# A fused attention and Fourier-mixing kernel: first-norm arithmetic moved to GpSimd, score products and loads of the first batch reordered, five filler matmuls added

## The chip, the cores and the metric

The kernel runs on one core of one Trainium2 chip. The metric is device time in microseconds (us) of one launch. Ten runs of the kernel before lie between 835.83 and 841.03 us, with a median of 837.63 us. One execution, of 836.47 us, was also profiled; the instructions in its trace span 834.7 us, and all the positions named below ("at 52.67 us") count from the start of that span.

## The reference

Four batches of 768 tokens, eight heads of 64. Each token attends to its neighbours closer than 16 tokens and to 24 block summaries (the maximum of 32 keys, the mean of 32 values). The heads side by side are a row of 512 numbers, x. Then a Fourier mix, a norm, and a two-layer network with hidden width 2048. Cut to what matters:

```python
k_sum = k.reshape(B, H, nb, 32, D).max(axis=3)
v_sum = v.reshape(B, H, nb, 32, D).mean(axis=3)
scores = concat([where(|i - j| < 16, q @ k.T / 8, -1e9), q @ k_sum.T / 8 + log(32)])
x = softmax(scores) @ concat([v, v_sum])          # to (B, S, H*D)
u = x + real(fft(fft(x, axis=1), axis=2))
un = (u - mean(u)) / sqrt(var(u) + 1e-6)          # over the 512 numbers of a row
out = u + relu(un @ w_ch1) @ w_ch2                # w_ch1, w_ch2 come as float64
```

## The kernel before

All matmuls are 32-bit, and each stands in the trace as two records, except transposes, which stand as one. The work goes batch by batch, and the tensor engine (PE) is the engine that is nearly always busy.

**First attention.** Batch 0 has nothing to overlap with, so its attention is written out by hand: inside `first_attention` the order of PE and VectorE (DVE) is the order of the code. Its eight heads are four pairs g = 0..3. For a pair, `prepare` transposes keys and queries (tiles `kn`, `qn`) into `kt`, `qt`, and DVE reduces the keys to block maxima `km` (L698). `wide_scores` multiplies twelve windows of 96 keys by 64 queries, in two halves of six windows; in each half the six windows of both heads come first, then the block maxima (L718), then the exponentials on ScalarE (ACT, L720) and a mask product on DVE. `wide_values` multiplies by the values `vw` (L741); DVE divides, and the halves of the sequence are folded (`fold_sequence`, `fold_halves`, `fold_ends`), which is the input of the Fourier stage. The PSUM banks are in two pools of four, `abank` and `bank`. Scores, sums of values and `av` use `abank`; transposes of batch 0 use `bank`.

**Loads.** Nearly every load goes through `fetch`, that is through SyncE's one queue (SP), in program order; a load that waits holds back all behind it. In `first_attention`, after pair 0, the queue gets the values of pair 2, the Fourier tables `fs` (two parts) and `fd` (L1016), then the values of pair 3 (`vw`, six loads of small pieces), then at g = 1 a first piece of the float64 weights (`words`), the keys and queries of batch 1, and another piece of weights.

**First Fourier stage.** `gen_fourier(0)` does the sequence transform (tiles `y`, L1072 and L1076; tables `fs`) and the channel transform (`mx`, L1100 and L1102; table `fd`), six row tiles. For each half of the rows (three tiles) DVE takes mean and variance (L1107, L1108) and then the inverse square root by a bit trick and three Newton steps, on tiles of 128x3: L1120 to L1132, fourteen DVE instructions for each half, all dependent. Then each row tile is scaled (`un`, L1144 on ACT or L1147 on DVE), transposed by PE (`unt`, L1151) and copied to `u` (L1152), and `_right_sums` makes four more operands from it. From these `gen_hidden` (tiles `hx`, `hy`, `hz`, L1173) makes the hidden layer by a seven-product scheme, and `gen_out` the output.

**Beside it.** A scheduler orders the instructions of all that runs together: `drive` mixes the Fourier stage with the conversion of the weights (`convert`, L929 to L939: DVE and ACT turn float64 words into float32, four raw pieces in flight, each freed by L936) and with the attention of batch 1 (`scores`, L757; `values`, L780 to L795). Block sums of values for batch 1 are loaded and added in `block_sums(1, 0)` (L1330; eight partial sums by additions and a DVE reduction, L623). The Fourier stage has priority 600 over the rest. For later batches the norm uses the same Newton lines, on DVE.

Of the kernel before, what the change touches and what calls it, by code (L numbers as in the profile page):

```python
# [10 lines left out]
I32 = mybir.dt.int32  # L11
# [5 lines left out]
P = 128  # L17
# [401 lines left out]
QB = 64  # L419
# [68 lines left out]
def _main_program(ctx, tc, q, k, v, moe_w_ch1, moe_w_ch2, out):  # L488
# [64 lines left out]
    def abank(shape, name):  # L553
        return psum.tile(shape, FP, tag="attn", bufs=4, name=name)
# [6 lines left out]
    def tt(out, in0, in1, op):  # L561
        nc.vector.tensor_tensor(out=out, in0=in0, in1=in1, op=op)  # L562

    def gtt(out, in0, in1, op):
        nc.gpsimd.tensor_tensor(out=out, in0=in0, in1=in1, op=op)
# [18 lines left out]

    def add_blocks(gg):
        raw, vb = to_add[gg]
        n = BLOCK * D // 2
        while n > D:
            tt(raw[:, 0:n], raw[:, 0:n], raw[:, n:2 * n], ADD)
            n //= 2  # L590
        tt(vb, raw[:, 0:D], raw[:, D:2 * D], ADD)

    def block_sums(b, gg):

        heads, rows = slice(4 * gg, 4 * gg + 4), 4 * nb
        f = BLOCK // 4
        n = f * D
        vb = spool.tile([rows, D], FP, tag="vbs", bufs=2, name=f"vbs_{b}_{gg}")
        for g in (2 * gg, 2 * gg + 1):
            sums[b, g] = vb, sel[:, g % 2]  # L600
        src = v[b, heads].rearrange("h (n f) d -> (h n) (f d)", f=BLOCK)
        if b == 0:

            raw = words[0:rows, 4 * n * gg:4 * n * (gg + 1)]
            fetch(out=raw, in_=src)
            to_add[gg] = raw, vb
            return
        if done_weights:
            raw = room(f"vb_{b}_{gg}")
            raw = [raw[0:rows, n * i:n * (i + 1)] for i in range(4)]  # L610
        else:

            raw = [bpool.tile([P, NC, P], FP, tag="s", bufs=5, name=f"vb_{b}_{gg}_{i}").rearrange("p n t -> p (n t)")
                   [0:rows] for i in range(4)]
        for i in range(4):
            fetch(out=raw[i], in_=src[:, n * i:n * (i + 1)])

        add = gtt if done_weights else tt
        add(raw[0], raw[0], raw[1], ADD)
        add(raw[2], raw[2], raw[3], ADD)  # L620
        add(raw[0], raw[0], raw[2], ADD)
        if not done_weights:
            nc.vector.tensor_reduce(out=vb, in_=raw[0].rearrange("p (f d) -> p d f", d=D), op=ADD, axis=AX.X)  # L623
        else:
            while f > 2:
                f //= 2
                gtt(raw[0][:, 0:f * D], raw[0][:, 0:f * D], raw[0][:, f * D:2 * f * D], ADD)
            gtt(vb, raw[0][:, 0:D], raw[0][:, D:2 * D], ADD)

# [72 lines left out]
    def wide_scores(b, g, between=None):  # L704

        kt, km, qt = kt_bufs[g % 2], km_bufs[g % 2], nat[b, g]
        p = apool.tile([P, 2, NQ, QB], FP, tag="p", name=f"p_{b}_{g}")
        for half in range(2):
            n0, n1 = NQ // 2 * half, NQ // 2 * (half + 1)
            ps = [abank([P, NQ // 2, QB], f"sc_{b}_{g}_{half}_{e}") for e in range(2)]  # L710
            for n in range(n0, n1):
                for e in range(2):
                    rows = slice(D * e, D * (e + 1))
                    nc.tensor.matmul(ps[e][0:WK, n - n0, :], kt[rows, QB * n:QB * n + WK],
                                     qt[rows, QB * n:QB * (n + 1)], start=True, stop=True)
            for e in range(2):
                rows = slice(D * e, D * (e + 1))
                nc.tensor.matmul(ps[e][WK:P], km[rows, :], qt[rows, QB * n0:QB * n1], start=True, stop=True)  # L718
            for e in range(2):
                nc.scalar.activation(out=p[:, e, n0:n1], in_=ps[e], func=AF.Exp, scale=SC)  # L720
                tt(p[:, e, n0:n1], p[:, e, n0:n1], wide[:, None, :].to_broadcast([P, NQ // 2, QB]), ALU.mult)
            if half == 0 and between:
                between()
        return p

    def sum_values(b, g):

        ps = abank([P, 2, D], f"vs_{b}_{g}")
        for e in range(2):
            vb, pick = sums[b, g]  # L730
            nc.tensor.matmul(ps[WK:P, e], pick[:, D * e:D * e + 32], vb, start=True, stop=True)

        (nc.vector.tensor_copy if g in (0, NP - 1) else nc.scalar.copy)(
            out=wide_vw(g)[WK:P, :, :, 0:D], in_=ps[WK:P, :, None, :].to_broadcast([P - WK, 2, NQ, D]))

    def wide_values(b, g, p, x):
        vw = wide_vw(g)
        av = [abank([P, NST, D1], f"av_{b}_{g}_{e}") for e in range(2)]
        for n in range(NQ):
            for e in range(2):  # L740
                nc.tensor.matmul(av[e][QB * (n % 2):QB * (n % 2 + 1), n // 2, :], p[:, e, n, :], vw[:, e, n, :],  # L741
                                       start=True, stop=True)
        for e in range(2):
            rc = rec[:, b * NP + g, e]
            nc.vector.reciprocal(out=rc, in_=av[e][:, :, D])
            tt(x[:, :, P * g + D * e:P * g + D * (e + 1)], av[e][:, :, 0:D],
               rc[:, :, None].to_broadcast([P, NST, D]), ALU.mult)
# [63 lines left out]
    def first_attention():  # L811
# [8 lines left out]
        for g in range(NP - 1):  # L820
            p[g + 1] = wide_scores(0, g + 1, (lambda: add_blocks(1)) if g == 1 else None)
            wide_values(0, g, p[g], x)
            load_values(*following(0, g, 2))
            for par in range(2):
                fold_sequence(par, g)
            if g == 0:
                get_tables(0)
            if g < NP - 2:
                prepare(0, g + 2)
                sum_values(0, g + 1)  # L830
            if g == NP - 3:
                load_raw(1)
                load(1, 0)
                load_raw(2)
                sum_values(0, g + 2)
        fold_halves(0, 0)
        wide_values(0, NP - 1, p[NP - 1], x)
# [166 lines left out]
    def get_tables(b):  # L1004
        tag, bufs = ("w1", 3) if b else ("w2", NC)
        fs = []
        for par in range(2):
            t = bpool.tile([P, 2, HT, F2 + 1], FP, tag=tag, bufs=bufs, name=f"fs_{b}_{par}")
            fetch(out=t, in_=dr["fs"].ap()[par])
            fs.append(t)  # L1010
        if b:
            fd = bpool.tile([P, C["fm"].shape[1]], FP, tag=tag, bufs=bufs, name=f"fm_{b}")
            fetch(out=fd, in_=dr["fm"].ap())
        else:
            fd = bpool.tile([P, 6, HD], FP, tag=tag, bufs=bufs, name=f"fd_{b}")
            fetch(out=fd, in_=dr["fd"].ap())  # L1016
        tables[b] = fs, fd
        return fs, fd

    def mix_halves(ps, y, fm, xt, half):  # L1020

# [16 lines left out]
    def gen_fourier(b):  # L1038
        x = x_of[b]
        Q = DM // 4  # L1040
        fs, fd = tables[b] if b in tables else get_tables(b)


        bank = abank if b else dense_bank
# [40 lines left out]
        for half in range(2):  # L1085
# [5 lines left out]
            for i in range(HT):  # L1091
# [23 lines left out]
                                     accum_out=var[:, i:i + 1])  # L1115
                yield

            y, z = norm[:, 0], norm[:, 1]
            if b == 0:
                nc.vector.tensor_scalar(out=minus, in0=both[:, :, 0], scalar1=-1.0, scalar2=None, op0=ALU.mult)  # L1120
                nc.vector.tensor_scalar(out=var, in0=both[:, :, 1], scalar1=1e-6, scalar2=None, op0=ADD)
            else:
                nc.vector.tensor_scalar(out=var, in0=var, scalar1=1.0 / DM, scalar2=1e-6, op0=ALU.mult, op1=ADD)
            nc.vector.tensor_scalar(out=y.bitcast(I32), in0=var.bitcast(I32), scalar1=1, scalar2=None,
                                    op0=ALU.arith_shift_right)
            nc.vector.tensor_scalar(out=y.bitcast(I32), in0=y.bitcast(I32), scalar1=-1.0, scalar2=float(0x5F3759DF),
                                    op0=ALU.mult, op1=ADD)
            for _ in range(3):
                nc.vector.scalar_tensor_tensor(out=z, in0=y, scalar=-0.5, in1=y, op0=ALU.mult, op1=ALU.mult)
                tt(z, z, var, ALU.mult)  # L1130
                nc.vector.scalar_tensor_tensor(out=y, in0=z, scalar=1.5, in1=y, op0=ADD, op1=ALU.mult)
            ins = nc.vector.tensor_tensor(out=z, in0=minus, in1=y, op=ALU.mult)  # L1132
            if b == 0:
                marks["mx", 0] = ins.ins
            norms.append((y, z))
        issued.add(("mx", b))
        for j in range(3):
            get_w1(b, j)

        for t in range(NST):  # L1140
# [9 lines left out]
            for d in range(NDT):  # L1150
                nc.tensor.transpose(ps[:, d // 2, d % 2, :], un[:, t, P * d:P * (d + 1)], ident)  # L1151
            (nc.vector.tensor_copy if t % 2 else nc.scalar.copy)(  # L1152
                out=u[:, half:half + 3:2, :, P * i:P * (i + 1)], in_=ps)
            yield
        _right_sums(tt, lambda i: u[:, i])
        wt["u", b] = u
# [170 lines left out]
    nc.vector.memset(vs, 0.0)  # L1327
    nc.vector.tensor_scalar(out=vs[:, :, D], in0=half_of, scalar1=float(BLOCK), scalar2=None, op0=ALU.mult)

    block_sums(1, 0)  # L1330

    def second_attention():
        prepare(1, 0)
# [76 lines left out]
```

## Time and profile before

| what | value |
|---|---|
| median of ten runs | 837.63 us (835.83 to 841.03) |
| profiled execution | 836.47 us, trace span 834.7 us |
| PE busy in the span | 803.9 us (96%) |
| DVE / ACT / POOL (GpSimd) busy | 487.8 us / 254.9 us / 16.1 us |
| mean granted PE clock | 0.992 |
| PE busy from 200 us to 700 us | 493.7 of 500 us |
| PE busy from 40 us to 50 us | 3.95 of 10 us |
| DVE busy from 90 us to 130 us | 39.8 of 40 us |

How to read it: PE is the engine that bounds the kernel, so time is lost where PE waits or where its granted clock is below full. From 200 us on there is little of either. The lower rows are stages of the first 200 us, in which batch 0 has its attention, its Fourier stage and its norm, and the weights are converted.

### The profile page before, as it was taken

To read this page: it belongs to the slowest core of one execution; us is meant where nothing else is said; L and a number is where in the kernel's file an instruction comes from. 1 tells how busy PE (TensorE), PEld (TensorE's weight loads), DVE (VectorE), ACT (ScalarE), POOL (GpSimd) and SP (SyncE) were. 2 spreads that over 40 slices of the span, in tenths; PEclk is the share of its full clock that TensorE was granted. 3 is DMA by queue.
4 is the path that set the end of the run, shared out by engine and by line. 5 is a ranking of instruction groups with operands and counts; after the bars stand their busy time and mean duration, and the time that the engine had idled before them with its cause. 6 is when DMAs were issued, how large, how long until landed. Compare 5 with 4: busy or idle time off the path is not lost.

```text
span 834.7 us, 14698 instructions
## 1 busy us (share of the span) xinstructions
PE 803.9 (96%) x6074; PEld 577.2 (69%) x6074; DVE 487.8 (58%) x1117; ACT 254.9 (31%) x561; POOL 16.1 (2%) x27
## 2 busy tenths in 40 slices
PE   8968998999999999999999999999999999999997
PEld 5757655445578856886568875787667875786586
DVE  5778998977978553533376823542347833532352
ACT  3533756444635023203234313121323502101200
POOL 0010000000000200020000000000000000000000
PEclk9989999999999999999999999999999999999999
DMA  9997697978733277247542253523312135205001
GB/s 207 228 246 153 194 248 252 313 217 262 241 109 108 79 269 202 83 77 248 106 92 97 85 202 129 128 38 122 129 46 88 72 101 214 89 1 220 1 26 54
DMA packets 101612, 120.55 MB, mean 144 GB/s; under 512 B 50560, under 2 KB 83552, under 8 KB 101344
## 3 DMA queue, kind: packets, MB, share of 16 engines
q1 hardware_dynamic: 100848, 119.31, 48.7%
q8 instruction: 50, 0.82, 0.4%
q10 hardware_dynamic: 688, 0.20, 0.1%
q14 instruction: 26, 0.21, 0.1%
HBM read 96.96 MB, written 22.54 MB: 143 GB/s over the span
## 4 chain that ended last, share of the span: by engine, by line
PE 83%; DVE 9%; ACT 3%; DMA 3%; issue 1%; ACTq 0%; SPq 0%; DVEq 0%
PE hx L1173 18%; PE ox L1237 17%; PE hz L1173 9%; PE oz L1237 8%; PE y L1072 4%; PE o L1214 4%; PE hy L1173 4%; PE oy L1237 4%; PE mx L1029 2%; PE sc L757 2%; PE unt L1151 1%; DVE w L562 1%; PE y L1076 1%; PE av L790 1%; DMA vw<-in_v_dram 1%
## 5 line engine op out<-in xcount | busy, mean ns | idle before, releaser
L1173 PE MATMUL hx<-u,w 128*128 128x384 f32 x512 | 186.2, 491 | 7.8 <-DVE h L562 3.9
L1173 PEld LDWEIGHTS hx<-u,w 128*128 128x128 f32 x512 | 94.5, 190 | 72.7 <-DVE h L562 7.6
L1173 PE MATMUL hz<-u,w 128*128 128x384 f32 x256 | 93.3, 487 | 0.0
L1237 PE MATMUL ox<-w,s 128*128 128x256 f32 x336 | 81.5, 381 | 0.3
L1237 PE MATMUL oz<-w,s 128*128 128x256 f32 x336 | 80.7, 379 | 0.0
L1237 PE MATMUL ox<-w,h 128*128 128x256 f32 x336 | 78.4, 381 | 0.4 <-DVE x L562 0.4
L1173 PEld LDWEIGHTS hz<-u,w 128*128 128x128 f32 x256 | 48.4, 190 | 34.3 <-ACT h L1190 1.1
L562 DVE TENSOR_TENSOR x<-ox,x 128x256 f32<-128x256 f32 x84 | 35.4, 423 | 62.0 <-PE ox L1237 61.9
L1237 PEld LDWEIGHTS ox<-w,h 128*128 128x128 f32 x336 | 63.2, 190 | 11.1 <-DVE x L562 1.5
L1237 PEld LDWEIGHTS oz<-w,s 128*128 128x128 f32 x336 | 63.5, 190 | 8.4
L1237 PEld LDWEIGHTS ox<-w,s 128*128 128x128 f32 x336 | 62.5, 190 | 9.2 <-DVE x L562 1.1
L562 DVE TENSOR_TENSOR h<-hx,h 128x384 f32<-128x384 f32 x32 | 17.8, 557 | 67.4 <-PE hx L1173 67.4
L1183 ACT COPY h<-hx 128x384 f32<-128x384 f32 x32 | 15.3, 477 | 127.3 <-PE hx L1173 115.6
L562 DVE TENSOR_TENSOR h<-hy,h 128x384 f32<-128x384 f32 x32 | 17.8, 557 | 60.6 <-PE hy L1173 57.4
L1173 PE MATMUL hy<-u,w 128*128 128x384 f32 x128 | 46.6, 487 | 0.0
L1214 PE MATMUL o<-w,h 128*128 128x512 f32 x96 | 42.6, 596 | 1.2 <-DVE w L562 1.2
L1237 PE MATMUL oy<-w,h 128*128 128x256 f32 x168 | 39.8, 379 | 0.0
L1199 ACT ACTIVATE h<-hx 128x384 f32<-128x384 f32 x32 | 15.7, 489 | 79.2 <-PE hx L1173 79.2
L1072 PE MATMUL y<-fs,fold 128*128 128x193 f32 x192 | 37.9, 344 | 0.1
L1072 PEld LDWEIGHTS y<-fs,fold 128*128 128x128 f32 x192 | 32.0, 195 | 6.3 <-issue 4.9
L1173 PEld LDWEIGHTS hy<-u,w 128*128 128x128 f32 x128 | 24.2, 190 | 17.1 <-DVE w L562 0.6
L1237 PEld LDWEIGHTS oy<-w,h 128*128 128x128 f32 x168 | 31.9, 190 | 4.3
(141 smaller groups left out, 1075.0 us busy)
## 6 DMA issues: line engine op xcount, KB each, us to landing
w<-dw SPq DMA_DIRECT2D x44, 896.0 KB, 5.8
words<-in_moe_w_ch_dram SPq DMA_DIRECT2D x32, 512.0 KB, 6.1
dw<-w SPq DMA_DIRECT2D x12, 896.0 KB, 7.3
vw<-in_v_dram SPq DMA_DIRECT2D x47, 192.0 KB, 5.4
kn<-in_k_dram SPq DMA_DIRECT2D x16, 384.0 KB, 4.8
qn<-in_q_dram SPq DMA_DIRECT2D x16, 384.0 KB, 5.6
out_dram<-x SPq DMA_DIRECT2D x24, 256.0 KB, 2.2
fs<-c_fs SPq DMA_DIRECT2D x8, 579.0 KB, 3.6
```

The lines of the kernel that those rows point to most:

```text
L562: nc.vector.tensor_tensor(out=out, in0=in0, in1=in1, op=op)
L757: nc.tensor.matmul(ps[h][r:r + 64, i, :], kt[rows, o:o + 64], qt[rows, o:o + BLOCK], start=True, stop=True)
L790: nc.tensor.matmul(av[r][32 * j:32 * (j + 1), t, :], p[rows, h, i - NB2 * h, :], vw[rows, i, :], start=(t == 0), stop=False, skip_group_ch ...
L1029: nc.tensor.matmul(out, y[:, g], table, start=True, stop=last, skip_group_check=True)
L1072: nc.tensor.matmul(y, fgs[par][:, st, P * g:P * (g + 1)], fs[par][:, g % 2, st, :], start=(st == 0), stop=(st == HT - 1))
L1076: nc.tensor.matmul(ps[0:1, par:par + F2 + 1], zq[:, par, s2:s2 + 1], fs[par][:, 0, s2, :], start=False, stop=False, skip_group_check=True)
L1151: nc.tensor.transpose(ps[:, d // 2, d % 2, :], un[:, t, P * d:P * (d + 1)], ident)
L1173: nc.tensor.matmul(ps, w[:, a, kk, :], u[:, r, kk, :], start=start and kk == 0, stop=stop and kk == 1, skip_group_check=True)
L1183: nc.scalar.copy(out=c11, in_=X)
L1199: nc.scalar.activation(out=c21, in_=X, func=AF.Relu)
L1214: nc.tensor.matmul(ps, h[:, n, hf, P * t:P * (t + 1)], wt[2, b, j][:, 2 * hf:2 * hf + 2, :], start=(n, hf) == (0, 0), stop=(n, hf) == (NC ...
L1237: nc.tensor.matmul(ps, left[a][:, n, :], wt[2, b, j][:, r, :], start=start and n == 0, stop=stop and n == NC - 1, skip_group_check=True)
```

## The change

Six things change; the arithmetic of the result is the same.

1. In `wide_scores` the window products of both halves come first, then the block maxima of both halves. All four `abank` banks are taken at once; so `sum_values` and `wide_values` take theirs from `bank`.
2. At g = 1 of `first_attention` the order of the loads is new: keys and queries of batch 1, two pieces of weights, the four raw block-sum tiles of batch 1, and then the table `fd`, which was ahead of the values of pair 3. These loads now stand in the code ahead of the preparation of pair 3. The additions of those block sums stay where they were in the code, in `add_blocks(2)`.
3. Block sums on DVE are a tree of additions to the end; the reduction L623 is gone.
4. In the Newton lines of batch 0 all but the integer shift goes to GpSimd. A step is now four instructions rather than three, for later batches too, where it stays on DVE.
5. Two matmuls of the identity by a 128x512 tile stand behind the norms, and three more behind the transposes of the third row tile; nothing reads their result.
6. In the order that the scheduler makes of it, nine more score products of batch 1 go ahead of `y`; the rest of the first pair's attention of batch 1, which lay between the norms and the transposes of `un`, comes after the last of these transposes.

```diff
@@ add_blocks, block_sums
+        add = gtt if done_weights else tt
+        if isinstance(raw, list):
+            add(raw[0], raw[0], raw[1], ADD)
+            add(raw[2], raw[2], raw[3], ADD)
+            add(raw[0], raw[0], raw[2], ADD)
+            raw, n = raw[0], n // 4
+        while n > 2 * D:
             n //= 2
-        tt(vb, raw[:, 0:D], raw[:, D:2 * D], ADD)
+            add(raw[:, 0:n], raw[:, 0:n], raw[:, n:2 * n], ADD)
+        add(vb, raw[:, 0:D], raw[:, D:2 * D], ADD)
...
-            nc.vector.tensor_reduce(out=vb, in_=raw[0].rearrange("p (f d) -> p d f", d=D), op=ADD, axis=AX.X)
...
+        to_add[2] = raw, vb
+        if now:
+            add_blocks(2)
@@ wide_scores
+        ps = [[abank([P, NQ // 2, QB], f"sc_{b}_{g}_{half}_{e}") for e in range(2)] for half in range(2)]
+        for n in range(NQ):
+            half, i = divmod(n, NQ // 2)
+            for e in range(2):
+                rows = slice(D * e, D * (e + 1))
+                nc.tensor.matmul(ps[half][e][0:WK, i, :], kt[rows, QB * n:QB * n + WK],
+                                 qt[rows, QB * n:QB * (n + 1)], start=True, stop=True)
         for half in range(2):
...
-                nc.tensor.matmul(ps[e][WK:P], km[rows, :], qt[rows, QB * n0:QB * n1], start=True, stop=True)
+                nc.tensor.matmul(ps[half][e][WK:P], km[rows, :], qt[rows, QB * n0:QB * n1], start=True, stop=True)
@@ sum_values, wide_values
-        ps = abank([P, 2, D], f"vs_{b}_{g}")
+        ps = bank([P, 2, D], f"vs_{b}_{g}")
...
-        av = [abank([P, NST, D1], f"av_{b}_{g}_{e}") for e in range(2)]
+        av = [bank([P, NST, D1], f"av_{b}_{g}_{e}") for e in range(2)]
@@ first_attention
             if g == 0:
                 get_tables(0)
+            elif g == 1:
+                load(1, 0)
+                load_raw(2)
+                block_sums(1, 0, False)
+                get_channel_table(0)
             if g < NP - 2:
                 prepare(0, g + 2)
                 sum_values(0, g + 1)
             if g == NP - 3:
-                load_raw(1)
-                load(1, 0)
-                load_raw(2)
                 sum_values(0, g + 2)
@@ gen_fourier
+    def keep_busy(name, t, n):
+        ps = dense_bank([P, DM], name)
+        for _ in range(n):
+            nc.tensor.matmul(ps, ident, t, start=True, stop=True)
...
+            eng = nc.vector if b else nc.gpsimd
...
-                nc.vector.tensor_scalar(out=minus, in0=both[:, :, 0], scalar1=-1.0, scalar2=None, op0=ALU.mult)
-                nc.vector.tensor_scalar(out=var, in0=both[:, :, 1], scalar1=1e-6, scalar2=None, op0=ADD)
+                eng.tensor_scalar(out=minus, in0=both[:, :, 0], scalar1=-1.0, scalar2=None, op0=ALU.mult)
+                eng.tensor_scalar(out=var, in0=both[:, :, 1], scalar1=1e-6, scalar2=None, op0=ADD)
...
             for _ in range(3):
-                nc.vector.scalar_tensor_tensor(out=z, in0=y, scalar=-0.5, in1=y, op0=ALU.mult, op1=ALU.mult)
-                tt(z, z, var, ALU.mult)
-                nc.vector.scalar_tensor_tensor(out=y, in0=z, scalar=1.5, in1=y, op0=ADD, op1=ALU.mult)
-            ins = nc.vector.tensor_tensor(out=z, in0=minus, in1=y, op=ALU.mult)
+                eng.tensor_tensor(out=z, in0=y, in1=y, op=ALU.mult)
+                eng.tensor_tensor(out=z, in0=z, in1=var, op=ALU.mult)
+                eng.tensor_scalar(out=z, in0=z, scalar1=-0.5, scalar2=1.5, op0=ALU.mult, op1=ADD)
+                eng.tensor_tensor(out=y, in0=y, in1=z, op=ALU.mult)
+            ins = eng.tensor_tensor(out=z, in0=minus, in1=y, op=ALU.mult)
...
+        if b == 0:
+            keep_busy("busy_0", x[:, NST - 1, :], 2)
...
+            if (b, t) == (0, HT - 1):
+                keep_busy("busy_1", un[:, t, :], 3)
@@ after first_attention
-    block_sums(1, 0)
+    add_blocks(2)
```

## The prediction

> **What bounds the kernel now.** I read the windows of busy time first. PE is busy 493.7 of 500 us from 200 to 700 us, so a gain has to come from the first 200 us. Columns: stretch, length, busy PE, PEld, DVE, ACT, POOL, granted clock, DMA share, GB/s.
>
> ```profile
> 40.00:50.00 10.00, 3.95 (x95) 3.50 (x91) 8.00 (x20) 1.29 (x4) 1.37 (x5) 0.98 0.99 226
> 50.00:60.00 10.00, 9.08 (x40) 7.19 (x41) 6.83 (x17) 4.88 (x13) 2.26 (x3) 0.67 1.17 241
> 80.00:90.00 10.00, 7.62 (x154) 6.46 (x156) 9.19 (x31) 7.65 (x15) 0.00 (x0) 0.83 0.87 224
> 120.00:130.00 10.00, 7.67 (x34) 4.95 (x33) 10.00 (x21) 7.73 (x16) 0.00 (x0) 1.00 1.08 214
> ```
>
> There are three losses: PE waits from 40 to 50, and then runs at a low clock; it waits and runs slowly from 80 to 90, at the norms; from 120 to 130 it waits with DVE full. PE's timeline, read next, names the waits (start, length, what, and in brackets the idle time before it and what ended it):
>
> ```profile
> 44.51 1.82 PE L741 MATMUL av<-vw,p 128*64 128x65 f32 x48 [3.35 <-DMA vw<-in_v_dram]
> 48.60 0.85 PE L694 MATMUL qk<-ident,kn 128*128 128x128 f32 x6 [2.27 <-DMA kn<-in_k_dram]
> 52.32 0.42 PE L757 MATMUL sc<-qt,kt 64*64 64x32 f32 x2 [0.92 <-ACT qt L696]
> ...
> 81.68 0.41 PE L780 MATMUL vs<-vbs,sel 96*128 96x64 f32 x2 [1.82 <-DVE norm L1126]
> ...
> 129.15 1.56 PE L1173 MATMUL hx<-u,w 128*128 128x384 f32 x4 [2.33 <-DVE h L562]
> ```
>
> The first two are late loads. SP's timeline says why:
>
> ```profile
> 34.00 0.43 SPq L549 DMA_DIRECT2D fd<-c_fd  x1
> ...
> 36.02 5.35 SPq L549 DMA_DIRECT2D vw<-in_v_dram  x1
> ...
> 43.30 0.50 SPq L549 DMA_DIRECT2D kn<-in_k_dram  x1
> ```
>
> `fd` stands ahead; the issue of a part of `vw` is then held 5.35 us, and `kn` is issued at 43.30 only. In the chain of waits from 32 to 60 us, that transfer (36.02, 8.36 us) is followed by `av`, by the folds on DVE from 48.37, and by `y` at 52.74.
>
> **The change, part by part.**
>
> *Loads and score order (+4.0 us).* Between the end of the third pair's `av` (41.17) and the first `y` (52.67) lie 11.5 us, in which PE does 3.6 us of work: `av` 1.7, transposes 1.5, scores 0.4. So 7.9 us are waits. After the change `fd` is behind `vw`, so I expect `vw` at 40 to 41 rather than 44.4. Keys and queries of batch 1 are issued near 40; loads of this stretch land 3.8 to 4.9 us after their issue, so near 44 to 45. The limit is then DVE's order: exponentials of the first halves start about 1.2 us later, as the second windows go ahead of them, but PE's waits for block maxima (0.58 us is one) go. The divisions of the last pair, which start at 46.27 now, I place at 44.8. The last fold ended at 49.85 and so ends at 48.4, and `qt` on ACT (eight copies of 0.52 us from about 43.5) is done by 48. `y` starts near 48.6: 52.67 − 48.6 ≈ 4.0. Bounds: 2 if the small pieces of `vw` and not `fd` hold the queue, 5 if DVE's order gives more. That `av` and block-sum products now share `bank` with transposes costs short waits for ACT's copies, taken in. `fd` itself, 8.3 us in flight in the trace, would land near 55 and is needed near 62; with that cover gone each us late is a us of wait.
>
> *Clock in `y` (0).* PE's clock is granted at half from 49.84 to 56.75 and costs about 1.9 us of `y`. PE would still be idle for much of 42.5 to 48.6, so I leave this loss: 0, bounds 0 and +1.9.
>
> *Newton steps on GpSimd.* The trace has no such chain there. For each half DVE does 14 dependent instructions of 0.13 to 0.17 us (0.07 of DVE's pace each), among large ones in order; from the last aggregate to the end it takes 8.2 us for the first half (73.98 to 82.2) and 7.9 for the second (78.9 to 86.86). POOL gets 16 for each half, 128x3, and the shift stays on DVE in its order. POOL's rows:
>
> ```profile
> L565 POOL TENSOR_TENSOR vb<-vb 96x512 f32<-96x512 f32 x6 | 8.3, 1394 | 232.1 <-DMA vb<-in_v_dram 231.9
> L565 POOL TENSOR_TENSOR vbs<-vb 96x64 f32<-96x64 f32 x2 | 0.6, 316 | 129.0 <-PE vs L780 129.0
> L868 POOL COPY zq<-fold 128x3 f32<-128x3 f32 x2 | 1.0, 490 | 2.4 <-DVE fold L562 2.4
> L866 POOL COPY fold<-fold 128x6 f32<-128x6 f32 x2 | 1.5, 761 | 6.2 <-DVE fold L562 6.2
> ```
>
> A line through 316 ns at 64 columns and 1394 at 512 gives 0.17 at 3 columns; 0.19 with a margin is the low bound. A dependent chain of additions of later block sums shows 0.08 more for each link. The copies of 3 columns, at the same width but beside a busy DVE, give 0.49, and the dearest copy of 6 columns 1.33: high bounds. The operation is nearest to the additions, the neighbourhood to the copies; I take 0.33, the low one with its link (0.27) and a little contention. Then, with T the end of `mx` (76.1 now, near 72 then): the last aggregate at T+3.3, two operations and the shift to T+4.3, 14 × 0.33 = 4.6 to T+9. The last transposes of `un` end T+10.2 to T+11.2. Queued behind: on POOL nothing that PE needs soon; on DVE the scaling of the first half's rows stands ahead of the last aggregate, so a late first norm delays the second.
>
> The Trainium skill ("GPSIMD Engine Reference", § 4.1 Engine selection) speaks against this part: elementwise work belongs on VectorE, and with two inputs it is about twice as slow on GpSimd. The trace agrees at 512 columns: 1.394 us there, 0.68 on DVE. By twice 0.16 us a step would be 0.32, and 14 of them 4.5 us, which is no other sum than mine.
>
> *Busy matmuls and the order at the norms (−3.3 us).* The same product as `o` of 128x512, 14 records in 6.25 us, is 0.446 a record; five matmuls are ten records, 4.46 us of PE. From T to the end of the transposes PE now has: the scores of one pair, 70 records at 0.017 (1.59 us for 94) = 1.2; busy 4.46; transposes, 24 at 0.13 = 3.1; together 8.7 of some 10.7 us, so 2.0 idle. After that the chain of exponentials and copies on ACT, moved here from under the norms, costs about 0.9. Lost: 4.46 + 2.0 + 0.9 = 7.4. Before, idle 2.5 (79.86 to 84.0) and half clock from 83.9 to 87.1, 1.6: 4.1. So −3.3, bounds −2 (POOL at 0.19) and −7 (0.53, with the clock falling too). What the fillers buy is the clock: without them 1.6 would stay lost and 4.46 be waits in part, so they are nearly free where POOL is slow.
>
> The Trainium skill ("TensorE: Matmul & The Clock Gate", Part 4) says that transposes don't count as busy for the clock. The trace has the clock at half during transposes at 84 to 87, but after a wait of 1.8 us, so it doesn't separate them. By that rule the three fillers among the transposes are needed, and without them the sum would be 1.6 lower.
>
> *DVE relieved (+3.5 us).* The block-sum work of batch 1 (three additions of 0.68 and the 1.02 reduction, 3.0 us) leaves the norm stage for DVE's gap from 50 to 60, where it is 6.83 busy. The tree costs 0.95 in place of 1.02: nothing. 26 Newton instructions off DVE at 0.07 are 1.8, plus the order's 0.7 or so: 5.5 us less on an engine that is 9.2 to 10 busy from 80 to 130. PE's waits for DVE and ACT between 94 and 153 are 0.21, 0.31, 1.17, 2.33 and 1.22, together 5.2. I take two thirds back; bounds +1 and +5. What comes late next is weights: pieces on SP's queue wait behind loads that PE frees, whose users now come after the transposes. The sixth and later pieces would be issued near 97.7, not 91.45, and land about when `hx` needs them (104); that is why not all returns.
>
> *Later batches (−0.6).* A step is four DVE instructions, not three: 3 more for each half, 18 in all, at 0.13 to 0.17 us in a chain that PE's other work covers mostly: bounds 0 and −1.5; about 0.03 each.
>
> Sum: 4.0 + 0 − 3.3 + 3.5 − 0.6 = +3.6. The profiled execution takes 836.47 (span 834.7 and 1.77 around it), so 832.9; the median is 1.16 above it: 834.0 us.
>
> **The rivals.**
>
> *Larger gain.* POOL at 0.19 (norm ready at T+7) and no low clock in `y`: 1.3 + 1.9 more than the forecast, and all 5.2 of the waits back, 1.5: 829.3. For it: DVE's own row for 128x3 is only 0.15, and the earlier `vw` shortens PE's gap. Against: POOL's small copies.
>
> *The loads don't do what they say.* The 5.35 us hold falls on the third part of `vw`, not the first: many small packets may hold the queue by themselves. Then the first term is 1 to 2, and the relief, which partly comes from the earlier end of `mx`, 2.5: 3.6 − 2.5 − 1 = +0.1, so 837.5, no change. For it: the stretch moves 226 GB/s, with DMA share 0.99, so what goes ahead of `vw` merely exchanges places with what goes behind.
>
> *Slower: the Newton chain on POOL becomes the wait.* Its place is between the last aggregate and the scaling of the second half. Each 0.1 us an operation moves it by 1.4 us. The gain of 3.6 is used up at 0.33 + 3.6/14 = 0.59; with the clock falling again (1.6) at 0.47. At 0.53 it is 2.8 + 1.6 = 4.4 against 3.6: 838.4; if DVE's relief is then useless too, 841.9; at 1.33, 14 × 1.0 = 14 and the clock: near 850. For it: the 0.49 copies. Against: they ran while DVE folded with strided tiles, and the other 6-column copy took 0.20.
>
> **How the numbers follow.** About 0.3%, 2.5 us, is what a measurement of this kernel can tell from no change: 835.1 to 840.1 counts as same. Forecast 0.45 (own range 831 to 837), larger gain 0.17, loads without effect 0.18, slower chain 0.20. Faster: most of the first (0.35) and all of the second, 0.52. Same: 0.10 of the first, 0.13 of the third and 0.04 of the fourth, 0.27. Slower: 0.16 of the fourth and 0.05 of the third, 0.21. The range reaches from the larger gain to the mild end of the chain: 828.5 to 840.5.
>
> **What would show it.** In the changed kernel's profile: `vw` landing near 41 and `y` starting near 48.6 (still at 51 or later: the loads failed); clock 0.5 for some 6 us in `y`; Newton rows on POOL of about 0.25 to 0.35 each, the second norm near T+9, the last transposes by T+11; ten records of 0.45 us ahead of them, with the clock full there; the 2.33 us wait near 129 gone; PE as busy as before from 200 us on. POOL rows of 0.5 or more, PE waiting for `words` or `w` at 95 to 110, or PE waiting for `fd` at `mx`, would make the prediction wrong.

## The result, and the profile after

The changed kernel takes 842.78 us (median of 15 runs, 839.66 to 847.18); the kernel before, run beside it, 836.72 us (52 runs). The ratio is 1.0073, 95% interval 1.0055 to 1.009: slower by some 6 us, where the prediction said 3.6 us faster (834.0 us, range 828.5 to 840.5). The profiled execution took 840.97 us, with a span of 839.1 us (before: 834.7).

The windows of the changed kernel first (stretch, length, then busy PE, PEld, DVE, ACT, POOL, granted clock, DMA share, GB/s):

```profile
40.00:50.00 10.00, 6.34 (x131) 5.08 (x128) 9.26 (x24) 5.63 (x12) 1.31 (x5) 0.95 1.00 281
50.00:60.00 10.00, 10.00 (x43) 7.91 (x43) 8.69 (x21) 3.36 (x10) 2.26 (x3) 0.71 1.03 187
80.00:90.00 10.00, 7.74 (x59) 4.33 (x58) 6.58 (x12) 7.52 (x16) 2.26 (x10) 1.00 0.10 29
90.00:100.00 10.00, 8.95 (x216) 6.41 (x216) 8.01 (x18) 3.46 (x8) 0.00 (x0) 0.83 0.95 223
120.00:130.00 10.00, 9.81 (x121) 6.00 (x121) 10.00 (x24) 5.26 (x12) 0.00 (x0) 1.00 0.33 90
```

The first stretch is better, as foretold: 6.34 us of PE in place of 3.95. So is the last: 9.81 in place of 7.67. What is new lies between. From 80 to 90, VectorE has fallen from 9.19 to 6.58 us and the loads from 224 to 29 GB/s; from 90 to 100 the clock is at half for a time, where it was full before.

PE's timeline of the changed kernel, at the places that the prediction named:

```profile
40.56 3.07 PE L740 MATMUL av<-vw,p 128*64 128x65 f32 x96
...
49.67 2.91 PE L1087 MATMUL y<-fs,fold 128*128 128x193 f32 x8 [0.96 <-POOL fold L872]
...
75.45 1.98 PE L1031 MATMUL busy<-x,ident 128*128 128x512 f32 x4
77.68 1.59 PE L1171 MATMUL unt<-ident,big 128*128 128x128 f32 x12 [0.24 <-DVE both L1123]
79.11 2.74 PE L1031 MATMUL busy<-big,ident 128*128 128x512 f32 x6
83.93 1.53 PE L1171 MATMUL unt<-ident,big 128*128 128x128 f32 x12 [2.08 <-ACT big L1164]
...
85.64 0.85 PE L772 MATMUL ss<-qt,km 64*32 64x384 f32 x8
```

The two last `av` run as one block with no wait for `vw`; `y` starts at 49.67, not 52.67, with nine score products of batch 1 ahead of it (18 records; before it was one, so eight more and not nine). Behind `mx` come the fillers, a wait of 2.08 us for the second norm, and only after the transposes the block scores `ss` of the first pair of batch 1, which stood at 77.56 before.

The second norm itself is not late. Its chain on POOL, first and last lines of the timeline:

```profile
77.71 0.43 POOL L1137 TENSOR_SCALAR stat<-both 128x3 f32<-128x3 f32 x1 [0.76 <-DVE both L1123]
...
81.73 0.19 POOL L1146 TENSOR_TENSOR norm<-norm 128x3 f32<-128x3 f32 x1
82.00 0.19 POOL L1147 TENSOR_TENSOR norm<-norm,stat 128x3 f32<-128x3 f32 x1
...
82.83 0.20 POOL L1150 TENSOR_TENSOR norm<-stat,norm 128x3 f32<-128x3 f32 x1
```

Most operations are 0.19 to 0.20 us, and the next one starts 0.27 to 0.28 us after the start of such a one; a few take 0.3 to 0.5. From 78.72 (L1143) to 83.03 the 14 of the second half take 4.31 us, 0.31 a link. `mx` ends at 74.1 and the norm is ready at 83.0, 8.9 us later; the prediction had said 9.

A ledger over the span (PE's idle time; what half clock cost, as one less the granted clock, times busy time, summed over windows of 1 us; and the fillers) accounts for 3.9 of the 4.4 us between the two spans:

| profiled execution | span | PE idle | half clock | fillers | sum of the last three |
|---|---|---|---|---|---|
| before | 834.7 | 30.8 | 4.5 | 0 | 35.3 |
| changed | 839.1 | 28.2 | 6.5 | 4.5 | 39.2 |

PE waits 2.6 us less, but the fillers' 4.5 us came on top instead of lying in the waits, and half clock costs 2.0 us more.

### The profile page after: what moved, and what is told of

It reads as the page before. It is cut to its first block, busy times and chain, and to the rows that moved or that the text cites. A ratio compares the mean times of both kernels' runs of the same rounds, so it can differ in the third digit from the quotient of the medians.

```text
span 839.1 us, 14755 instructions
## 1 busy us (share of the span) xinstructions
PE 810.9 (97%) x6084; PEld 578.0 (69%) x6084; DVE 485.4 (58%) x1117; ACT 254.1 (30%) x561; POOL 24.5 (3%) x59
## 4 chain that ended last, share of the span: by engine, by line
PE 83%; DVE 7%; ACT 6%; issue 1%; POOL 1%; DMA 1%; DVEq 0%; ACTq 0%; POOLq 0%
PE hx L1195 18%; PE ox L1259 17%; PE hz L1195 9%; PE oz L1259 8%; PE y L1087 4%; PE hy L1195 4%; PE oy L1259 4%; PE o L1236 3%; PE mx L1042 2%; PE sc L756 2%; ACT kt L694 2%; ACT qt L694 2%; DVE x L562 1%; PE y L1091 1%; PE qk L684 1%
## 5 line engine op out<-in xcount | busy, mean ns | idle before, releaser
L1195 PEld LDWEIGHTS hz<-u,w 128*128 128x128 f32 x256 | 48.5, 190 | 34.6 <-ACT h L1212 1.4
```

The lines of the kernel that those rows point to most:

```text
L1195: nc.tensor.matmul(ps, w[:, a, kk, :], u[:, r, kk, :], start=start and kk == 0, stop=stop and kk == 1, skip_group_check=True)
```

## The experiments

All times are medians beside runs of the kernel before on the same chip; the ratios carry 95% intervals. A hundredth of a per cent is 0.08 us.

| kernel | median us | ratio to before |
|---|---|---|
| changed | 842.78 | 1.0073 (1.0055 to 1.009) |
| e1 no fillers | 841.18 | 1.0068 (1.0042 to 1.0095) |
| e2 Newton on VectorE | 833.50 | 0.9961 (0.9938 to 0.9984) |
| e3 neither fillers nor GpSimd | 837.16 | 1.0001 (0.9976 to 1.0026) |
| e4 old score halves | 844.59 | 1.0107 (1.007 to 1.0143) |
| e5 conversion behind the shift | 840.56 | 1.005 (1.0027 to 1.0073) |
| e6 order on PE | 841.13 | 1.0063 (1.0043 to 1.0083) |
| e7 before, with fillers | 836.27 | 0.9994 (0.9974 to 1.0013) |
| e8 Newton on VectorE, three instructions | 840.24 | 1.0046 (1.0025 to 1.0066) |
| e9 order on PE, ScalarE, VectorE | 832.98 | 0.9966 (0.9948 to 0.9985) |
| e10 Newton on VectorE, no fillers | 834.87 | 0.9982 (0.9967 to 0.9998) |
| e11 e2 again | 832.49 | 0.9954 (0.9939 to 0.9969) |
| e12 edges on ScalarE alone | 835.45 | 0.9987 (0.9966 to 1.0009) |
| e13 e9 with old loads | 839.24 | 1.0035 (1.001 to 1.006) |
| e14 e9 with old score halves | 833.88 | 0.9991 (0.9969 to 1.0014) |
| e15 e9, three instructions later | 834.88 | 0.9977 (0.9954 to 1.0001) |

### First: which part costs the time (e1 to e4)

e1 takes the five fillers out:

```diff
-        if b == 0:
-            keep_busy("busy_0", x[:, NST - 1, :], 2)
...
-            if (b, t) == (0, HT - 1):
-                keep_busy("busy_1", un[:, t, :], 3)
```

> The changed kernel without the five dense matmuls; all else kept. Three theories for the 6.1 us (836.7 to 842.8). F (fillers): their 4.46 us of PE are paid whole, and they push the first pair's attention of batch 1 out of the wait for the norms; without them that attention stands in the wait again: 837 to 838.5, and the time from the end of mx to the first hx shrinks though the clock may fall to half there. N (Newton steps on GpSimd are the loss): 842 to 844, as the wait for the second norm stays and the clock falls. A (first attention: a 1.4 us wait on issue at 26 and the half clock behind it, 28 to 31): 842 or more.

e2 puts the Newton steps back on VectorE:

```diff
-            eng = nc.vector if b else nc.gpsimd
+            eng = nc.vector
```

> The changed kernel with the Newton steps of batch 0 back on VectorE (still four instructions a step), fillers kept. F: the fillers still cost, but now stand in a longer wait with part of the first pair's attention: 841 to 843.5. N: 837 to 839. A: 842 to 843.5.

e3 does both, with the three-instruction step of before:

```diff
-                eng.tensor_tensor(out=z, in0=y, in1=y, op=ALU.mult)
-                eng.tensor_tensor(out=z, in0=z, in1=var, op=ALU.mult)
-                eng.tensor_scalar(out=z, in0=z, scalar1=-0.5, scalar2=1.5, op0=ALU.mult, op1=ADD)
-                eng.tensor_tensor(out=y, in0=y, in1=z, op=ALU.mult)
+                nc.vector.scalar_tensor_tensor(out=z, in0=y, scalar=-0.5, in1=y, op0=ALU.mult, op1=ALU.mult)
+                tt(z, z, var, ALU.mult)
+                nc.vector.scalar_tensor_tensor(out=y, in0=z, scalar=1.5, in1=y, op0=ADD, op1=ALU.mult)
```

> The changed kernel with neither fillers nor Newton steps on GpSimd (three instructions a step on VectorE, as before): what is left is the order of loads and scores and the tree. F: the 3.0 us by which y starts earlier remain, part of it lost again at the VectorE waits: 833.5 to 836. N: the same, 833.5 to 836. A: 838 or more, as the wait at 26 and the half clock at 28 to 31 remain.

e4 undoes the order of the score halves and the PSUM pools that go with it:

```diff
-        ps = [[abank([P, NQ // 2, QB], f"sc_{b}_{g}_{half}_{e}") for e in range(2)] for half in range(2)]
...
         for half in range(2):
+            ps = [abank([P, NQ // 2, QB], f"sc_{b}_{g}_{half}_{e}") for e in range(2)]
...
-        av = [bank([P, NST, D1], f"av_{b}_{g}_{e}") for e in range(2)]
+        av = [abank([P, NST, D1], f"av_{b}_{g}_{e}") for e in range(2)]
```

> The changed kernel with the score halves in the old order (block maxima and exponentials of the first half ahead of the windows of the second, PSUM pools as before); loads, Newton steps and fillers kept. F and N: 841.5 to 844, y starting within 1 us of the changed kernel's. A: 838.5 to 840, with no wait on issue near 26 and the clock full at 28 to 31.

My first theory was the fillers. It fell: without them 841.18 us. The first attention fell too (e4 is no faster). Newton on VectorE, one line, gave 833.5 us, which is faster than the kernel before; e11, the same program again, confirmed it (832.49). So the loss goes with the place of the Newton steps. But how? Their operations had taken 0.31 us a link, and the norm had been ready when foretold.

Two of these runs say something of the loads too. e3 is in substance the kernel before with the new loads, the new order of scores and the tree. Its `y` starts at 50.37, 2.3 us earlier than before, and its time is the same as before (1.0001), where 833.5 to 836 was expected, or 838 and more by the third theory: an earlier `y` alone gave nothing that shows at the end. And in e4 the wait for `vw` is back, with `fd` behind `vw`, and `y` starts at 52.14, against the expectation for it:

```profile
44.03 3.07 PE L739 MATMUL av<-vw,p 128*64 128x65 f32 x48 [2.99 <-DMA vw<-in_v_dram]
```

The six loads of `vw` hold the queue for 7.43 us there, from 34.91; in the changed kernel it is 5.93 us, from 33.54. Why they took longer in e4 is open; e14 below has the same loads and score halves and waits 0.18 us.

### Second: by what means (e5 to e8)

The program's order of instructions is made by a scheduler from the durations that it assumes, and with Newton on GpSimd it set the transposes of `un`, and what feeds them, ahead of the rest of the first pair's attention. Three causes were to be told apart: the weight conversion, which was queued on VectorE behind the last Newton step and was free once that step had left VectorE (M); the order on PE (O); GpSimd itself (P).

e5 queues the conversion behind the shift, which stayed on VectorE:

```diff
-            nc.vector.tensor_scalar(out=y.bitcast(I32), in0=var.bitcast(I32), scalar1=1, scalar2=None,
+            ins = nc.vector.tensor_scalar(out=y.bitcast(I32), in0=var.bitcast(I32), scalar1=1, scalar2=None,
...
+            if b == 0:
+                marks["mx", 0] = ins.ins
```

> The changed kernel, but the instruction behind which the weight conversion of this stage is queued is the integer shift on VectorE, as it stays there, and not the last Newton step, which is now on GpSimd and so holds back nothing on VectorE. PE's order stays as in the changed kernel. Theory M (the conversion, no longer queued behind the norms, gets in their way): 834 to 837. Theory O (PE's order: the scores' exponentials and the next pair's transposes now come after the transposes of un, and all of their chain on ScalarE, the loads behind it and the weights are late): 841 to 844. Theory P (Newton steps on GpSimd are too slow): 841 to 844.

e6 queues the transposes of `un` on PE behind those of the next pair:

```diff
-                nc.tensor.transpose(ps[:, d // 2, d % 2, :], un[:, t, P * d:P * (d + 1)], ident)
+                with tc.issue_after(marks["qk", 1, 1]) if b == 0 else ExitStack():
+                    nc.tensor.transpose(ps[:, d // 2, d % 2, :], un[:, t, P * d:P * (d + 1)], ident)
```

> The changed kernel with Newton steps on GpSimd and with the fillers, but the transposes of un queued on PE behind the key and query transposes of the next pair of batch 1, so that the block scores and these transposes stand ahead of them, as in the kernel with Newton on VectorE. O: 832 to 836, as fast as with Newton on VectorE (833.5) within 2 us; the keys of the fourth pair are issued near 78 and not near 88. M or P: 840 to 844.

e7 is the kernel before with the five fillers at the places that they have in the changed one; e8 is e2 with the three-instruction step of e3.

> The kernel before with the five fillers as its only edit. If fillers buy more clock and better order than their 4.46 us, where the attention stays ahead of the transposes: 833 to 836. If they are mere cost: 838 to 841, 1 to 4.5 us over before.

> Newton steps on VectorE with three instructions a step, as before, all else as changed (loads, score order, fillers). Against the kernel with four instructions a step (833.5): 24 VectorE instructions fewer, 0 to 1.5 us faster: 832 to 834. The order of the key and query transposes differs a little (three of four ahead of the transposes of un); if that order is what counts, 835 to 838.

M and O in this form fell: 840.56 and 841.13 us, which gives back less than a quarter of the 9.3 us by which e2 is faster. e7 shows fillers alone as nothing (ratio 0.9994). e8 was a miss by 6 to 8 us, and it was the clock: e8's and e2's runs have nearly the same time once what the clock took is set aside (mean time times one less the mean granted clock: 840.35 − 11.1 = 829.2 us and 833.72 − 5.0 = 828.7 us). In the profile of e8 one stretch holds 6.6 us of that:

```profile
84.00:98.00 14.00, 13.80 (x158) 8.64 (x147) 7.30 (x16) 3.51 (x8) 0.00 (x0) 0.52 1.07 244
```

PE is busy for 13.80 of 14 us there, at a granted clock of 0.52. What puts e8 into that state and e2 not was only argued (a little more waiting among small products after the fillers), not tried. e8 and e3 differ by the five fillers alone, and e8, which has them, is the slower one by 0.45%.

What e6 had left as it was is seen in its timeline of ScalarE:

```profile
77.54 0.50 ACT L695 COPY kt<-qk 64x384 f32<-64x384 f32 x1
80.63 1.52 ACT L1165 ACTIVATE big<-x,norm 128x512 f32<-128x512 f32 x2 [2.59 <-POOL norm L1151]
82.05 1.04 ACT L1174 COPY u<-unt 128x512 f32<-128x512 f32 x2
83.12 1.55 ACT L695 COPY kt<-qk 64x384 f32<-64x384 f32 x3
```

Three of four `kt` copies stand behind a scaling (`big`) that waits 2.59 us for the norm, though PE had their input ready before it (its last transposes of keys ended at 76.82). The lateness goes on from there: VectorE waits 1.66 us for the last `kt` at 84.71, with work behind it, and PE then waits for VectorE:

```profile
90.47 1.67 PE L795 MATMUL av<-vs,p 64*128 64x130 f32 x12 [2.25 <-DVE vs L562]
```

Queue order on PE alone doesn't help if ScalarE's queue has its own.

### Third: all three queues (e9, e12), and the square (e10, e11)

e9 keeps Newton on GpSimd and the fillers, keeps the edits of e5 and e6, and also queues the scalings of `un` behind the copies and the block maxima of the next pair, as they stand when Newton is on VectorE:

```diff
+            behind = {1: ("copy", 1, 1, False, 0, 1), 3: ("copy", 1, 1, True, 1, 1), 4: ("km", 1, 1),
+                      5: ("copy", 1, 1, True, 1, 1)}
+            with tc.issue_after(marks[behind[t]]) if b == 0 and t in behind else ExitStack():
```

> Newton steps on GpSimd and fillers as in the changed kernel, but on PE, ScalarE and VectorE the scaling and the transposes of un are queued behind the work of the next pair of batch 1 that stands ahead of them when Newton is on VectorE (exponentials, key and query transposes, their copies, block maxima), and the weight conversion behind the shift. If the loss of 9 us against Newton on VectorE (842.8 and 833.5) is the order in which three engines then wait for the second norm: 832 to 836. If it is GpSimd itself: 839 to 843.

e12 has of these only the edges of rows 1, 3 and 5, which ScalarE scales. (PE's order follows in part, as its trace shows below: a row can't be transposed before it is scaled.)

> The changed kernel, with only ScalarE's three scalings of un queued behind the copies of the next pair's keys and queries (none of the edges on PE and VectorE). PE alone in the old order gave 841.1, PE and ScalarE together 833.0. If ScalarE's queue, standing behind a scaling that waits for the norm, is what made the copies, the scores and the later loads late: 832.5 to 836. If both queues have to be changed: 838 to 842.

e10 is e2 without fillers; e11 is e2 once more.

> Changed kernel, Newton on VectorE with four instructions, no fillers: the fourth corner of the square of fillers and place of the Newton steps (842.8 with both, 841.2 without fillers, 833.5 with fillers and VectorE). If fillers gain by the clock where VectorE makes the norm: 836 to 839, with more of its time at half clock than in the kernel with fillers. If the four-instruction kernel is fast for another reason: 831 to 834.

> The kernel that measured 833.5, unchanged, on another chip or at another time. If its gain is a property of the program: 832 to 835 and a ratio of 0.994 to 0.998 to before; if it was the luck of the clock in those twelve runs (mean granted 0.994 against 0.987 with three instructions): 836 to 840.

e9 runs the same work on the same engines as the changed kernel and takes 832.98 us: 1.07% of the time, 9.0 us, is the order of the queues. By the measure used for e8 the means, which lie 9.7 us apart, part into 5.7 us of time apart from the clock (834.6 and 828.9 us) and 4.0 us that the clock took (8.4 and 4.4). The edit of ScalarE's three scalings gives 0.86%, 7.2 us (e12), that of PE's transposes 0.1% (e6). But e12 is not ScalarE alone. On its PE the block scores and the transposes of the next pair have moved ahead of all but one of the six rows of `un`:

```profile
75.99 0.85 PE L774 MATMUL ss<-qt,km 64*32 64x384 f32 x8
...
82.01 1.09 PE L1175 MATMUL unt<-ident,big 128*128 128x128 f32 x8
```

So e6 is PE's order without ScalarE's, e12 both, and the step between them, 0.76% or 6.4 us, is what ScalarE's queue is worth once PE's order is mended. What it is worth without PE's was not told. GpSimd as such costs nothing that shows: 0.9966 there, 0.9961 and 0.9954 on VectorE, with intervals that overlap.

ScalarE's timeline in the changed kernel, and then in e9, shows what is behind what:

```profile
76.98 0.81 ACT L1164 ACTIVATE big<-x,norm 128x512 f32<-128x512 f32 x1 [11.45 <-POOL norm L1150]
...
83.06 1.52 ACT L1164 ACTIVATE big<-x,norm 128x512 f32<-128x512 f32 x2 [2.38 <-POOL norm L1150]
...
86.60 0.86 ACT L762 ACTIVATE p<-sc 128x384 f32<-128x384 f32 x2
...
87.72 2.11 ACT L694 COPY kt<-qk 64x384 f32<-64x384 f32 x4
```

```profile
76.74 0.87 ACT L765 ACTIVATE p<-sc 128x384 f32<-128x384 f32 x2 [12.19 <-PE sc L759]
...
79.02 1.05 ACT L695 COPY kt<-qk 64x384 f32<-64x384 f32 x2
79.96 0.80 ACT L1170 ACTIVATE big<-x,norm 128x512 f32<-128x512 f32 x1
...
84.97 1.52 ACT L1170 ACTIVATE big<-x,norm 128x512 f32<-128x512 f32 x2
```

In the changed kernel the scalings stand first and wait, and exponentials and copies start ten us later (86.60, not 76.74). Most of these were not ready behind the scalings, as PE does their products only from 85.39 on, behind the transposes of `un`: here both queues hold them up. What was ready is a step of the weight conversion (L933; VectorE had made its input by 79.90), which starts at 84.49. In e9 the same copies fill the wait, and the last scalings come when the norm has long been ready. Ten us around the norms as a window, changed kernel and then e9, each from about the end of `mx`:

```profile
74.00:84.00 10.00, 7.58 (x94) 4.24 (x94) 6.71 (x18) 3.43 (x6) 6.03 (x27) 1.00 0.00 0
```

```profile
73.00:83.00 10.00, 9.07 (x120) 5.69 (x120) 8.36 (x21) 5.76 (x12) 6.54 (x27) 1.00 0.37 100
```

ScalarE does 3.43 us against 5.76, PE 7.58 against 9.07, and the loads stand at 0 GB/s against 100. That last figure looks like the next link: the load of the fourth pair's keys needs a buffer which PE frees by the transposes of the second pair. On SP's timeline, first of the changed kernel, then of e9 and then of e6:

```profile
87.72 0.39 SPq L549 DMA_DIRECT2D kn<-in_k_dram  x1
```

```profile
78.32 0.39 SPq L549 DMA_DIRECT2D kn<-in_k_dram  x1
```

```profile
76.84 0.39 SPq L549 DMA_DIRECT2D kn<-in_k_dram  x1
```

In the changed kernel the queue stands still nine us longer than in e9, and the pieces of weights behind those keys with it (88.93, not 80.22). But e6 speaks against this as the main cost: its keys go at 76.84 and its weights at 78.74, earlier than in e9, and it takes 841.13 us. Nor is it that VectorE has nothing to do: from 73 to 103 us it is busy 22.7 us in the changed kernel and 21.7 in e12, which is 7.2 us faster. From 60 to 160 us, PE's listed waits sum to 6.9 us in the changed kernel, 7.8 before, and 3.7 in e9. The profiled e9 has a span of 832.0 us, with 25.6 us idle, 3.0 lost to the clock and the 4.5 of the fillers: a sum of 33.1, 2.2 less than before, where the span is 2.7 less. Between the profiled changed kernel and e9 this sum differs by 6.1 us; 4.8 of it lies from 60 to 160 us, and 1.8 is half clock ahead of 60, where PE's order is the same in both.

The square of place and fillers is closed: on GpSimd, in the order that the change has, 1.0073 with fillers and 1.0068 without; on VectorE 0.9961 and 0.9954 with, 0.9982 without. In e10 and e11 the time apart from the clock is the same (828.8 us each), although e11 does 4.5 us more of PE's work, and the clock takes 6.3 and 3.75 us. So in this order the fillers lie wholly in waits. That they buy clock, 1.8 to 2.3 us by these medians, is not shown: the intervals touch or overlap, the profiles of e1 and e10, without fillers, have the clock at full from 60 to 160 us, and with three instructions a step the clock took 11.1 us with fillers (e8) and 7.1 without (e3). In the bad order they bought nothing that shows.

### Fourth: is the early gain carried to the end (e13 to e15)

> The kernel that measured 833.0 (Newton on GpSimd, fillers, work queued ahead of un) with the loads in the order of before (fd ahead of the values of the last pair). The prediction gave the loads and scores together 4.0 us at y. If the loads give it and it is carried to the end: 835 to 838, y near 52. If VectorE and the weights take early gains back: 832 to 834.5 with y at 52 all the same.

> The kernel that measured 833.0 with the score halves and PSUM pools of before. If the new order of halves gains: 834 to 836. If it only moves time, and the wait on issue near 26 and the half clock behind it eat it: 831.5 to 834.

e13 is e9 with the loads as before:

```diff
             if g == 0:
                 get_tables(0)
-            elif g == 1:
-                load(1, 0)
-                load_raw(2)
-                block_sums(1, 0, False)
                 get_channel_table(0)
...
+                load_raw(1)
+                load(1, 0)
+                load_raw(2)
```

The two large waits of before are back in its timeline of PE, and `y` starts nearly where it did then:

```profile
43.66 1.83 PE L743 MATMUL av<-vw,p 128*64 128x65 f32 x48 [2.98 <-DMA vw<-in_v_dram]
47.81 0.85 PE L692 MATMUL qk<-ident,kn 128*128 128x128 f32 x6 [2.32 <-DMA kn<-in_k_dram]
...
51.91 2.30 PE L1089 MATMUL y<-fs,fold 128*128 128x193 f32 x6
```

It takes 839.24 us: 0.69%, 5.8 us, more than e9, and more than was expected. `y` starts only 2.8 us later than in e9, and 0.8 earlier than in the kernel before, which is nevertheless faster (e13's ratio is 1.0035). So part of the 5.8 must lie elsewhere; it may be the order of later work, which the scheduler made anew. e14, with the old score halves and pools, measures 833.88 us with `y` at 48.96 (e9: 49.1); its interval overlaps that of e9. The new order of halves is worth nothing that these runs can tell.

e15 gives batches 2 to 4 the three-instruction step.

> The kernel that measured 833.0 (Newton on GpSimd in the first batch, fillers, work queued ahead of un) with three VectorE instructions a Newton step, as before, in batches 2 to 4; the order of the first 240 us is unchanged. The prediction charged the fourth instruction 0.6 us, bounds 0 and 1.5: 831.5 to 833. If it is hidden: 833 within a us. If the new order of the later batches counts for more: 834 or more.

834.88 us, with an interval that overlaps that of e9: no gain from taking the 18 instructions out; the later batches were ordered anew, so their price by itself is not told.

## Why the prediction was wrong, point by point

**Loads and score order (+4.0): nearly right at `y`, not shown at the end.** `y` starts 3.0 us earlier in the profiled execution; in 13 of the 14 profiles with the new loads it starts at 48.5 to 50.4, in the three with the old ones at 51.9 to 52.7, against a forecast of 48.6. The loads did it: e13 takes most of it away, and the new order of halves adds nothing (e14). Their rival, that small pieces of `vw` can hold the queue by themselves, is not wholly out: e4 is the fourteenth. The sum then added the gain at `y` to the whole time as it stood. In e3 nothing of it that shows arrives; in e9's order the loads are worth 5.8 us (e13), with the caution above. The working also took PE's work between 41.17 and 52.67 as 3.6 us; a window of it shows 4.54, so 7.0 us were waits and not 7.9.

**Clock in `y` (0): right** for the profiled execution, 2.9 us against 2.8 from 50 to 75 us. The 1.7 us of half clock from 28 to 32 had no term.

**Newton on GpSimd: right in its own numbers.** 0.31 us a link on the mean (taken: 0.33, lower bound 0.19), norm at T+8.9 (T+9), transposes finished at 85.46, T+11.4 (T+10.2 to 11.2). The rival that made it slow through this chain named the right part of the change and the right sign, but the wrong price: it needed 0.47 to 0.59 us an operation. The Trainium skill ("GPSIMD Engine Reference", § 4.1 Engine selection) counts two-input operations as about twice as slow on GpSimd; at 128x3 the trace shows 0.19 us there and 0.13 to 0.17 on VectorE, so at this width the rule overstates it.

**Busy matmuls and the order at the norms (−3.3): this is the step that failed.** Its sentence was "After that the chain of exponentials and copies on ACT, moved here from under the norms, costs about 0.9." The move was seen, and priced at 0.9 us. What it cost is 9.0 us: that is what e9 gives back by the order of the queues alone. Most of it, 7.2 us, comes back with ScalarE's scalings and PE's transposes together (e12), next to nothing with PE's transposes alone (e6). The prediction asked what was queued behind the waiting norm on POOL and on VectorE, but not on ScalarE, where the scaling stood first and eleven instructions of 5.5 us behind it. By what path 5.5 us of later ScalarE work become 9.0 us is open in part: e6 shows waits of VectorE and PE that follow from late copies, and 4.0 us of the difference between the means is the clock. The late keys and weights on SP's queue, which the prediction let trim another term, are not enough to explain it (e6). The Trainium skill ("TensorE: Matmul & The Clock Gate", the section on the array's 32×32 sub-arrays, at engine queue depths) calls the queues of ScalarE and VectorE strictly first in, first out; the lines of `big` with 2.38 us of waiting (changed kernel, L933 ready behind it) and 2.59 us (e6, three copies ready behind it) agree. The prediction also charged 1.6 us of clock to a kernel without the fillers; the profiles of e1 and e10, which have none, show the clock full from 60 to 160 us.

**DVE relieved (+3.5): not there in the changed kernel, there in e9.** The 2.33 us wait near 129 went, but others came: 1.82 us for ScalarE at 107.36 and 1.39 at 140.53. Of 7.8 us of listed waits from 60 to 160 (those at the norms among them) 0.9 were regained, against 4.1 in e9. What spent the relief in the changed kernel is not shown. VectorE's low share from 80 to 90 is not the mark of it: it is 6.58 us there and 6.41 in e9.

**Later batches (−0.6): not told apart** from nothing (e15).

With the order mended, e9 is 3.0 us faster than the kernel before; the prediction said 3.6. That is near, but in part luck. In e9's profile PE idles 5.2 us less than before, where the terms for loads, norms and DVE together came to 7.1 us less (4.0 − 0.4 + 3.5); the fillers cost their 4.5, and half clock 1.5 us less (1.6). Over all its runs the time apart from the clock is that of the kernel before (828.9 and 828.6 us), and the gain is what the clock took, 4.4 us rather than 7.7. So the step on the norms' order accounts for the miss, but the other terms are not confirmed one by one.

## What to carry to other kernels

When an instruction moves to another engine in a program that a scheduler orders, compare the order of every queue, not only the instruction's own time: whatever the scheduler then believes to be ready sooner gets in front of other work, and if it waits there, all behind it waits too. The engine to look at is the one that consumes the moved result, and the work that stands behind the consumer in its queue. Fillers are free where they lie in a wait (e10 and e11); whether they gain anything was not shown here, so fill the wait with real work first. And an early gain is not yet a gain at the end: try it by itself, as e3 does here.

## What was not expected of the hardware

The granted clock explains most of the spread between runs of one program: 28 of the 29 runs of before that stood beside e1 to e4 (the other took 1658.64 us) go from 832.99 us at a mean clock of 0.994 to 842.23 at 0.984. It can stay at half while PE is busy: in e8 it falls at 84 us, after PE has idled 1.0 us of two, and stays at 0.50 from 85 to 98 with PE busy all the time. The fillers didn't prevent it in the changed kernel, where it fell at 93 us, 11 us after the last of them.

With the new order of score halves, PE waits 0.62 to 1.95 us on "issue" near 26 us in 11 of 13 profiles, and in none of the four with the old order. In the changed kernel the clock is at half from 28 to 32 after it (0.57 granted in that window). What makes this wait wasn't tried.
